# Two forward layers and their backward on one core: attention scores of four heads in one stretch instead of two pairs

## The chip, the core and the metric

The kernel runs on one core of a Trainium2 chip. A core has five engines with queues of their own: PE (TensorE, matrix products into PSUM), DVE (VectorE), ACT (ScalarE, exponentials and copies), POOL (GpSimd) and SP, which here only issues DMAs. PSUM holds eight banks of 512 float32 values on each of 128 partitions; PE writes it, DVE and ACT read it, POOL can't. The metric is the device time of the whole program in microseconds (us); lower is better.

## What is computed

The reference runs four layers on one sequence of 2048 tokens with 640 features and 32 heads of 20 features, then the gradients of everything.

```python
x = x + A(layernorm(x), A_wqkv, A_wo)      # linear attention, phi(t) = (t > 0 ? t + 1 : exp(t)) + 1e-6
x = x + B(layernorm(x), B_wqkv, B_wo)      # causal softmax attention, window of 256 tokens
x = x + A(layernorm(x), A_wqkv, A_wo)
x = x + B(layernorm(x), B_wqkv, B_wo)
out, vjp = jax.vjp(f, x, weights); return (out, *vjp(grad_out))
```

In layer B a token attends to itself and the 255 tokens before it: `scores = q k^T * 20 ** -0.5`, masked, softmax, times `v`. The change touches the forward part only.

## The kernel before

**Tiles.** A tile is 128 tokens, so there are 16. Heads are padded to 32 rows: the transposed queries and keys (`QT`, `KT`) hold four heads on the 128 partitions, 32 rows each, and eight such groups (`G = 8`). A tile's queries meet the keys of at most three tiles (`nkt`): its own block, where the mask is a triangle, the one before, unmasked, and the oldest, where the mask is the other triangle. For the first tile `nkt` is 1, for the second 2.

**Passes.** `forward()` records all its operations, each with an engine, an assumed duration, and what it reads and writes; a list scheduler (`Sched.order`) then puts them into a fixed order for each engine, by the assumed durations, a priority (the order in which they were recorded), and rings of buffers. The order is settled when the kernel is built; on the chip each engine takes its queue in order and waits at semaphores. After the first layer's chunks (`a_first(items, 0, 0)`) come two passes over all tiles, `ab_pass(0, False)` and `ab_pass(2, True)`. In one pass a tile goes through the linear-attention product (`a_num`, line 613 and the 32-column products of line 420), its output projection, a layer norm, the six query/key/value chunks of layer B (`b_qkv`), attention (`attn`), and layer B's output projection. The first pass also computes four of the six chunks of the next layer A for each tile, so it has 14 chunks a tile, the second 10. A chunk is five matmuls of 128 x 128 x 320 (line 420) into one PSUM bank of the ring `mm`, copied or added out by DVE or ACT.

**Late q.** Between the passes `late_q` computes the two query chunks of the next layer A (line 523), as fillers, with an exponential (line 528), a minimum and a maximum-plus-add on DVE (529, 531).

**Attention** works on pairs of heads. For each of 16 pairs in a tile, `products` issues 2 x `nkt` matmuls that use 32 rows of PE each (`tile_position`, line 690) into a buffer of two PSUM banks, one per head; `weights` takes one exponential over both heads (line 697, ACT), masks the own block on POOL (line 700), and the oldest block on POOL for the second pair of a group (line 704) and on DVE, by a product with `maskT_first`, for the first (line 708). `values` multiplies with the values (line 731, 2 x `nkt` matmuls of 32 columns) into a bank shared by 16 heads, which DVE normalises (738, 739).

**PSUM.** Eight banks: three single ones in ring `mm`, two buffers of two banks in ring `s`, one in `pv`. In layer 0's first stage ring `s` also takes transposes and two of the six chunks, a whole buffer each. The masked weights `e` have five buffers of two heads.

**Recording order.** The values of a pair are recorded a lag behind its scores: 2.1 sixteenths of a tile in the first pass and 3.1 in the second (`spread` in `ab_pass`).

**Copies.** Of the six chunks of layer B, ACT copies three (line 665) and DVE three (663); of the value chunks of layer A ACT copies one (476) and DVE one (479).

**Backward.** `bwd_phase` and `B_attn_bwd` follow; they use `ckv`, a small constant, at line 1495. Behind the forward the order of instructions on each engine is the same in both kernels, but for two memsets of `ckv`.

Of the kernel before, what the change touches and what calls it, by code (L numbers as in the profile page):

```python
# [11 lines left out]
ALU = mybir.AluOpType  # L12
# [188 lines left out]
class Kern:  # L201
    def __init__(self, ctx, tc, x0, A_wqkv, A_wo, B_wqkv, B_wo, grad_out, outs):
# [45 lines left out]
        self.maskT_last = self.const.tile([P, P], BF, name="maskT_last")  # L248
        self.maskT_first = self.const.tile([P, P], BF, name="maskT_first")
# [4 lines left out]
        self.mask_steps = [keep(self.maskT_last, 0, [[1, P]], -1), keep(self.maskT_first, -1, [[-1, P]], 1)]  # L254
# [8 lines left out]
        for t in (self.bmask, self.hmask, self.maskT_last, self.maskT_first):  # L263
            nc.vector.memset(t, 1.0)
        self.ckv = self.const.tile([P, 3, 4 * DH], F32, name="ckv")
        nc.vector.memset(self.ckv[:, 0:2, :], self.c_att)
        nc.vector.memset(self.ckv[:, 2, :], 1.0)
# [69 lines left out]
    def forward(self):  # L337
# [5 lines left out]
        with ExitStack() as st:  # L343
# [5 lines left out]
            def ring(name, n, shape, dt=BF, **kw):  # L349
# [4 lines left out]
            mmp, sp_ = pool("mm_ps", 3, **PS), pool("s_ps", 2, **PS)  # L354
            R = dict(
                s=Ring(2, make=lambda: sp_.tile([P, 2, 512], F32, name="s_ps"), name="s_ps"), pv=ring("pv_ps", 1, [P, 16, 32], F32, **PS),
                mm=Ring(3, make=lambda: mmp.tile([P, 512], F32, name="mm_ps"), name="mm_ps"),
                e=ring("e_sb", 5, [P, 2, 3, P]), QT=ring("QT", 2, [P, G, P]), KT=ring("KT", 5, [P, G, P]),
# [64 lines left out]
            def turn(how, dst, src, n, r, w):  # L423
# [5 lines left out]
                if how == "s":  # L429
                    ps.make = lambda: sp_.tile([P, 16, P], BF, name="s_ps")  # L430
                else:
                    ps.make = lambda: mmp.tile([P, 8, P], BF, name="mm_ps")
# [27 lines left out]
            def a_qkv(l, tt, hnT):  # L460
# [3 lines left out]
                def chunk(ci):  # L464
                    def f():
                        kind, c0 = "qkv"[ci // 2], ci * CW
                        o = c0 - ci // 2 * D
                        ring = "s" if l == 0 and ci in (0, 2) else "mm"
                        ps = R[ring].buf()
                        if ring == "s":  # L470
                            ps.make = lambda: sp_.tile([P, 1024], F32, name="s_ps")
                        mm_chunk(ps, CW, [(lambda k=k: hnT.t[:, k, :], lambda k=k: wsb["Wqkv_A"][:, k, c0:c0 + CW],
                                           k == 0, k == DT - 1) for k in range(DT)], [key_of(hnT), ("Wqkv_A", ci)])
                        if kind == "v":
                            if ci == 4:
                                op("ACT", av(CW), lambda: nc.scalar.copy(vv[:, tt, o:o + CW], ps.t[:, 0:CW]), [ps],
                                   [("vv", tt, ci)])
                            else:
                                op("DVE", vp(CW), lambda: nc.vector.tensor_copy(vv[:, tt, o:o + CW], ps.t[:, 0:CW]),
                                   [ps], [("vv", tt, ci)])  # L480
                                dma("ACT", lambda: self.tm_view(sv["v"])[:, tt, :], lambda: vv[:, tt, :], 160 * KB,
# [1145 lines left out]
```

## Time and profile before

| | us |
|---|---|
| median of 3 runs | 2318.53 (2316.77 to 2324.01) |
| span of the profiled execution | 2322.2 |
| PE busy in that span | 2109.3 (91%) |
| DVE busy | 1455.2 (63%) |
| ACT busy | 1240.5 (53%) |
| POOL busy | 853.2 (37%) |
| forward passes, first exponential of line 697 to the last one's start | 145.7 to 435.6, and 504.3 to 760.7 |

The profile shows one execution, some microseconds apart from the runs' median. Times in it are counted from the span's start. In a table of windows each row has the stretch, its length, the busy time of each engine with its instructions in brackets, the granted PE clock (1.00 is full speed), the share of time in which the 16 DMA engines were busy, and GB/s. In a timeline a row has the start, the duration of equal instructions in a row, the engine, the line, the operation, what it writes and reads, and in square brackets the idle time before it and what ended it. In a list of waits a row has who waited for whom, the total in us, how often, and the longest.

### The profile page before, as it was taken

The numbers are of one execution on the slowest core, as the hardware profiler recorded it, in microseconds if no ns is written. First come the engines' busy times: TensorE is split into PE (matmuls) and PEld (weight loads), VectorE is DVE, ScalarE is ACT, GpSimd is POOL, SyncE is SP. The second block draws the span as 40 slices with busy tenths as digits, with TensorE's granted clock in tenths as the row PEclk, the third lists the DMA queues.
The fourth block names the chain that finished last, engine by engine and source line by source line (L and its number), as shares of the span: only waits on it lengthen the run. The fifth ranks groups of instructions, "written<-read, shape, count | busy, mean of one in ns | idle before, by whom it ended". The sixth has DMA issues, their size and how long they took to land. (4 is left out here: it accounts for less than half of the span.)

```text
span 2322.2 us, 69222 instructions
## 1 busy us (share of the span) xinstructions
PE 2109.3 (91%) x28146; PEld 1435.7 (62%) x28146; DVE 1455.2 (63%) x3089; ACT 1240.5 (53%) x2077; POOL 853.2 (37%) x1852
## 2 busy tenths in 40 slices
PE   6989999989999888989889989998899888997899
PEld 4646666655555557777756557746777775654664
DVE  6756666555554678899833439805989994443551
ACT  4638888437888158888722213314888881210330
POOL 1015555215566345555512203303555551220110
PEclk9989999889999889999999999999999999998999
DMA  7759989366776956767788789936677678878973
GB/s 258 223 129 205 207 203 201 114 168 150 158 151 172 222 138 125 134 122 135 145 179 178 175 168 211 192 104 130 125 133 131 127 145 167 191 162 188 190 154 100
DMA packets 937073, 377.93 MB, mean 163 GB/s; under 512 B 817072, under 2 KB 921136, under 8 KB 936496
## 3 DMA queue, kind: packets, MB, share of 16 engines
q1 hardware_dynamic: 856672, 299.45, 63.4%
q10 hardware_dynamic: 80080, 74.06, 10.1%
q8 instruction: 220, 3.60, 0.7%
q14 instruction: 101, 0.83, 0.1%
HBM read 115.34 MB, written 114.95 MB: 99 GB/s over the span
## 5 line engine op out<-in xcount | busy, mean ns | idle before, releaser
L1442 ACT ACTIVATE e_sb<-pair 128x768 bf16<-128x768 f32 x480 | 389.3, 812 | 112.9 <-PE pair L1422 105.5
L1457 DVE TENSOR_TENSOR ds_sb<-pair,e_sb 128x768 bf16<-128x768 f32 x480 | 436.3, 948 | 6.6 <-POOL e_sb L1446 6.6
L697 ACT ACTIVATE e_sb<-s_ps 128x768 bf16<-128x768 f32 (+2 forms) x512 | 383.8, 772 | 98.9 <-PE s_ps L690 47.0
L700 POOL TENSOR_SCALAR_AFFINE_SELECT e_sb<-e_sb 128x256 bf16<-128x256 bf16 x512 | 223.9, 438 | 451.0 <-ACT e_sb L697 436.9
L931 PE MATMUL mm_ps<-wq,dqT 128*128 128x320 bf16 x1920 | 285.5, 304 | 20.7 <-DMA dqT<-dqkv 20.1
L931 PEld LDWEIGHTS <-om 128*128 128x128 bf16 x1920 | 190.9, 100 | 171.3 <-DMA om<-o 13.4
L1449 POOL TENSOR_SCALAR_AFFINE_SELECT e_sb<-e_sb 128x256 bf16<-128x256 bf16 x448 | 182.6, 408 | 264.4 <-ACT e_sb L1442 256.0
L931 PE MATMUL mm_ps<-dqkv,om 128*128 128x480 bf16 x1280 | 272.2, 371 | 0.0
L1102 POOL TENSOR_TENSOR gw<-w,gcar 128x640 f32<-128x640 f32 x64 | 89.5, 1399 | 478.7 <-ACT w L1099 468.8
L931 PEld LDWEIGHTS <-dqT 128*128 128x128 bf16 x1920 | 186.9, 99 | 97.8 <-DMA dqT<-dqkv 22.9
L1446 POOL TENSOR_SCALAR_AFFINE_SELECT e_sb<-e_sb 128x256 bf16<-128x256 bf16 x512 | 207.3, 408 | 73.0 <-ACT e_sb L1442 71.7
L1084 ACT ACTIVATE dh<-mm_ps 128x320 f32<-128x320 f32 x128 | 56.0, 437 | 331.4 <-PE mm_ps L931 268.9
L1470 PE MATMUL dsT_ps<-ident,ds_sb 128*128 128x128 bf16 x2244 | 192.8, 223 | 29.2 <-ACT dsT L1474 25.4
L1474 ACT COPY dsT<-dsT_ps 128x768 bf16<-128x768 bf16 x240 | 191.0, 796 | 12.2 <-PE dsT_ps L1470 6.0
L1470 PEld LDWEIGHTS <-ds_sb 128*128 128x128 bf16 x2244 | 140.1, 99 | 92.5 <-issue 89.0
L690 PE MATMUL s_ps<-QT,KT 32*128 32x128 bf16 x2880 | 172.0, 222 | 8.7 <-ACT e_sb L697 5.8
L420 PE MATMUL mm_ps<-Wqkv_B,hnTB 128*128 128x320 bf16 x960 | 178.7, 306 | 0.5 <-DMA hnTB<-hnB 0.5
L1486 PE MATMUL dqvk_ps<-Ksl,dsT 128*128 128x32 bf16 x2160 | 167.3, 177 | 3.5 <-DVE dqkv L1495 3.0
L1486 PEld LDWEIGHTS <-dsT 128*128 128x128 bf16 x2880 | 156.1, 97 | 22.4 <-issue 21.8
L1490 PE MATMUL dqvk_ps<-Qsl,ds_sb 128*128 128x32 bf16 x2160 | 165.0, 176 | 0.0
L1490 PE MATMUL dqvk_ps<-dOsl,e_sb 128*128 128x32 bf16 x2160 | 165.0, 176 | 0.0
L690 PEld LDWEIGHTS <-KT 32*128 32x128 bf16 x2880 | 85.0, 94 | 117.7 <-issue 111.4
(184 smaller groups left out, 3937.6 us busy)
## 6 DMA issues: line engine op xcount, KB each, us to landing
qkvp<-qk_slab SPq DMA_DIRECT2D x32, 512.0 KB, 3.3
o<-o SPq DMA_DIRECT2D x64, 160.0 KB, 3.3
om<-o SPq DMA_DIRECT2D x20, 512.0 KB, 5.0
hn<-hn SPq DMA_DIRECT2D x64, 160.0 KB, 3.0
om<-hn SPq DMA_DIRECT2D x20, 512.0 KB, 5.0
qkvp<-v_slab SPq DMA_DIRECT2D x32, 256.0 KB, 2.5
dOpt<-slab ACTq DMA_DIRECT2D x32, 256.0 KB, 3.4
Ksl<-qkvp SPq DMA_DIRECT2D x12, 512.0 KB, 4.6
```

The lines of the kernel that those rows point to most:

```text
L690: nc.tensor.matmul(s.t[:, i, j * P:(j + 1) * P], lhsT=kTs[j].t[r, g, :], rhs=qT.t[r, g, :], start=True, stop=True, tile_position=(HPAD * h ...
L697: op("ACT", av(2 * nkt * P), lambda: nc.scalar.activation(e.t[:, :, 0:nkt, :], s.t[:, :, 0:nkt * P].rearrange("p h (i q) -> p h i q", q=P) ...
L700: op("POOL", 410, lambda: nc.gpsimd.affine_select(out=e.t[:, :, nkt - 1, :], in_=e.t[:, :, nkt - 1, :], compare_op=ALU.is_ge, fill=0.0, ba ...
L931: nc.tensor.matmul(ps.t[:, w0:w0 + width], lhsT=lhsT(), rhs=rhs(), start=start, stop=stop)
L1442: nc.scalar.activation(e, PR[h][:, :, 0:3 * P].rearrange("p i (j q) -> p i j q", q=P), ACT.Exp, scale=self.c_att)
L1446: nc.gpsimd.affine_select(out=e[:, :, j, :], in_=e[:, :, j, :], compare_op=ALU.is_ge, fill=0.0, base=0, pattern=[[0, 2], [-1, P]], channel ...
L1449: nc.gpsimd.affine_select(out=e[:, :, j, :], in_=e[:, :, j, :], compare_op=ALU.is_ge, fill=0.0, base=-1, pattern=[[0, 2], [1, P]], channel ...
L1457: nc.vector.tensor_mul(DS[n][:, hs], PR.pop(h)[:, :, 0:3 * P].rearrange("p i (j q) -> p i j q", q=P), E[n][:, hs])
L1470: nc.tensor.transpose(ps[:, i, j, :], DS[n][:, 2 * p + i, j, :], self.ident)
L1474: (nc.vector.tensor_copy if h % 2 else nc.scalar.copy)(TSB[h], TPS.pop(h))
L1486: nc.tensor.matmul(a[:, 0, hh, :], lhsT=TSB[2 * n + hh // 2][:, hh % 2, j, :], rhs=ld[g]["K"][:, k, cs], start=(i == 0), stop=(i == len(dq ...
L1490: nc.tensor.matmul(a[:, 1 + x, hh, :], lhsT=src[n][:, hh, j, :], rhs=ld[g][rhs][:, q, cs], start=(i == 0), stop=(i == len(dkv) - 1))
```

## The change

Scores of all four heads of a group are issued in one stretch of 4 x `nkt` matmuls. Three heads go into one tile of three banks (`s3`, one buffer), the fourth into a single bank (`s1`, two buffers). The exponential is split: one over three heads, one over the fourth. All masks are on POOL: own block for three heads, own block for the fourth, oldest block for all four. `maskT_first` and `maskT_last` go. The ring `mm` has two banks instead of three; in layer 0's first stage the five banks of `s3` and `s1` serve as five single buffers, for three of six chunks. The weights have three buffers of four heads. ACT's copies of layer B's chunks move to DVE, as does the one of layer A's value chunk except in layer 0. `late_q` works chunk by chunk with a single bank each. The lag is 3.1 sixteenths in both passes. `ckv` is made after the forward.

```diff
-            mmp, sp_ = pool("mm_ps", 3, **PS), pool("s_ps", 2, **PS)
+            mmp = pool("mm_ps", 2, **PS)
+            sb = pool("s3_ps", **PS).tile([P, 3, 512], F32, name="s3_ps")
+            sa = [pool(f"s1_ps{i}", **PS).tile([P, 512], F32, name=f"s1_ps{i}") for i in range(2)]
+            singles = [sb[:, 0, :], sb[:, 1, :], sb[:, 2, :]] + sa
...
-                e=ring("e_sb", 5, [P, 2, 3, P]), ...
+                s=Ring(5, tiles=singles, name="s"), s3=Ring(1, tiles=[sb], name="s3"),
+                s1=Ring(2, tiles=sa, name="s1"), pv=ring("pv_ps", 1, [P, 16, 32], F32, **PS),
+                mm=Ring(2, make=lambda: mmp.tile([P, 512], F32, name="mm_ps"), name="mm_ps"),
+                e=ring("e_sb", 3, [P, 4, 3, P]), ...
...
-                            if ci == 4:
+                            if ci == 4 and l == 0:
...
-                ps, e, p_ = R["s"].buf(), R["ee"].buf(), R["pp"].buf()
+                e, p_ = R["ee"].buf(), R["pp"].buf()
                 for ci in range(2):
+                    ps, c0 = R["s1"].buf(), ci * CW
...
-                        if ci % 2:
-                            op("DVE", vp(CW), lambda: nc.vector.tensor_copy(out(), src()), [ps, "zeros"], [key])
-                        else:
-                            op("ACT", av(CW), lambda: nc.scalar.copy(out(), src()), [ps, "zeros"], [key])
+                        op("DVE", vp(CW), lambda: nc.vector.tensor_copy(out(), src()), [ps, "zeros"], [key])
...
+                def scores(g):
+                    def f():
+                        s3, s1 = R["s3"].buf(), R["s1"].buf()
+                        def mm_s():
+                            for j in range(nkt):
+                                for hh in range(4):
+                                    r = slice(HPAD * hh, HPAD * (hh + 1))
+                                    out = s3.t[:, hh, :] if hh < 3 else s1.t
+                                    nc.tensor.matmul(out[:, j * P:(j + 1) * P], lhsT=kTs[j].t[r, g, :], rhs=qT.t[r, g, :],
+                                                     start=True, stop=True, tile_position=(HPAD * hh, 0))
+                        op("PE", 200 + 56 * nkt, mm_s, [qT] + kTs, [s3, s1])
+                        e = es[g] = R["e"].buf()
+                        op("ACT", av(3 * nkt * P), lambda: nc.scalar.activation(
+                            e.t[:, 0:3, 0:nkt, :], s3.t[:, :, 0:nkt * P].rearrange("p h (i q) -> p h i q", q=P),
+                            ACT.Exp, scale=self.c_att), [s3], [(e, 0, j) for j in range(nkt)])
+                        op("ACT", av(nkt * P), lambda: nc.scalar.activation(
+                            e.t[:, 3, 0:nkt, :], s1.t[:, 0:nkt * P].rearrange("p (i q) -> p i q", q=P),
+                            ACT.Exp, scale=self.c_att), [s1], [(e, 1, j) for j in range(nkt)])
...
+                        op("POOL", 530, lambda: own_block(0, 3), [], [(e, 0, nkt - 1)])
+                        op("POOL", 300, lambda: own_block(3, 4), [], [(e, 1, nkt - 1)])
+                        if nkt == 3:
+                            op("POOL", 640, oldest_block, [], [(e, 0, 0), (e, 1, 0)])
...
-                           [(e, j) for j in range(nkt)] + [(v, c) for v in vts for c in (4, 5)], [pv])
+                           [(e, i, j) for i in range(1 + p_) for j in range(nkt)] + [(v, c) for v in vts for c in (4, 5)], [pv])
...
-                        lag = 0.001 + part * (3.1 if last else 2.1) / (2 * G)
-                        spread(items, tt + lag, tt + lag + 1.0, [att(i, part) for i in range(2 * G)])
+                        lag = 0.001 + part * 3.1 / (2 * G)
+                        spread(items, tt + lag, tt + lag + 1.0, [att(i, part) for i in range((1 + part) * G)])
```

More of the change, by code (lines that the diff above doesn't have):

```diff
@@ L467, in f @@
                         o = c0 - ci // 2 * D
[L468 to L471, printed above, removed]
+                        ps = R["s" if l == 0 and ci in (0, 2, 4) else "mm"].buf()
                         mm_chunk(ps, CW, [(lambda k=k: hnT.t[:, k, :], lambda k=k: wsb["Wqkv_A"][:, k, c0:c0 + CW],
@@ L749, in values @@
                     return f
[L750 to L751 removed]
+                return [scores(g) for g in range(G)], [values(g, p_) for g in range(G) for p_ in (0, 1)]
             def spread(items, t0, t1, fs):
```

88 lines of the change are left out of this document (31 added, 57 removed).

## The prediction

> **What bounds the kernel now.** I read the profile page's span first, then busy times over two long stretches of full tiles, then who waited for whom there, then one timeline. The change touches the two forward passes, so everything is read from those.
>
> ```profile
> span 2322.2 us, 69222 instructions
> ```
>
> ```profile
> core 0: us, PE busy (x) PEld busy (x) DVE busy (x) ACT busy (x) POOL busy (x), PEclk, DMA share, GB/s
> 212.00:398.00 186.00, 185.22 (x2713) 113.46 (x2711) 124.29 (x355) 152.83 (x260) 98.75 (x240) 1.00 0.93 204
> 420.00:437.00 17.00, 15.87 (x186) 9.28 (x183) 6.68 (x19) 12.10 (x19) 8.36 (x21) 0.52 0.13 41
> 552.00:715.00 163.00, 160.79 (x2528) 96.54 (x2527) 93.27 (x269) 134.09 (x210) 98.10 (x240) 1.00 0.71 155
> ```
>
> The first and third stretch hold 160 of the L697 exponentials each, 16 to a tile: a tile takes 18.6 us in the first pass and 16.3 in the second. PE is busy for all of it at full clock; ACT follows with 82%. The waits of PE in the same two stretches are next to nothing, 0.7 us in ten tiles and 1.7 in ten:
>
> ```profile
> PE s_ps L690 <- ACT e_sb L697: 0.7, 2, 0.4
> ```
>
> ```profile
> PE s_ps L690 <- ACT e_sb L697: 1.7, 5, 0.5
> ```
>
> So PE alone sets these tiles. The timeline shows what on it is not arithmetic:
>
> ```profile
> 266.07 0.84 PE L420 MATMUL mm_ps<-Wo_B,oTB 128*128 128x320 bf16 x5
> ...
> 266.84 0.34 PE L690 MATMUL s_ps<-QT,KT 32*128 32x128 bf16 x6
> ...
> 267.11 0.31 PE L731 MATMUL pv_ps<-v_slab,e_sb 128*128 128x32 bf16 x6
> ...
> 267.27 0.84 PE L420 MATMUL mm_ps<-Wqkv_B,hnTB 128*128 128x320 bf16 x5
> 267.28 0.81 ACT L697 ACTIVATE e_sb<-s_ps 128x768 bf16<-128x768 f32 x1 [0.38 <-PE s_ps L690]
> ```
>
> A chunk of three 320-column matmuls lasts 0.57 at 259.84, one of five 0.84: 0.135 each, 0.675 for five. The scores should thus start at 266.745; they start at 266.84, **0.10 late**. Six of them last 0.34, one alone 0.22 (its mean on the page), so the last starts 0.12 after the first: 0.06 for each pair of row groups. The values start 0.27 after the scores, so 0.15 after the last. One stretch costs 0.10 + 0.12 + 0.15 = 0.37, of which some 0.2 is switching. Check: 16 x 0.37 scores, 16 x 0.16 values (267.11 to 267.27), 14 chunks x 0.675, 0.6 for the linear-attention products = 18.5; with ten chunks 15.8. Measured 18.6 and 16.3.
>
> **The change, part by part.** *Scores.* Two stretches of six become one of twelve. If four row groups run as the pairs do, its three steps cost the same 0.06 each: 0.10 + 0.13 + 0.15 = 0.38 instead of 0.74, 0.36 less. If only two ever run together, six steps: 0.55, 0.19 less. The trace has no four groups; I take 0.38, because the pair's two matmuls start within 0.01 us and each has a PSUM bank of its own, as the four will. A tile gains 8 x 0.36 = 2.9 us (bounds 1.5 to 2.9): PE alone would give 15.65 and 12.95. The Trainium skill (TensorE: Matmul & The Clock Gate, Measured speedup vs the span model) has four row tiles at 3.07 times one, not 4. By that the three steps cost some 0.06 more, 0.5 us a tile, an estimate, and the sum below would be 11 us smaller; no run here shows it yet.
>
> *Exponentials.* L697 takes 812 ns for 768 columns, 597 for 512, 385 for 256: 172 + 0.834 a column. 1152 columns: 1.13; 384: 0.49. Neighbours overlap (two lie in 1.52 us at 745.80, 0.10 less than the sum), so 1.13 + 0.39 replaces 2 x 0.71, nothing in sum. Leaving ACT are three copies of L665 a tile (0.43 each), and L476 in the first pass; DVE takes them at 0.47 and loses eight L708 of 0.30: -0.5 us a tile in the first pass, -1.0 in the second, so cost nothing while DVE, busy for two thirds, covers them.
>
> *Masks.* POOL takes 409 ns for 256 columns and 295 for 128 (L252): 523 for 384, 637 for 512. A group costs 1.46 instead of 3 x 0.41; 11.7 us a tile, under the period but in the chain.
>
> *The new chain.* Before, four banks in two buffers let the next scores start while an exponential ran. Now there is one three-bank buffer: the next scores wait for the three-head exponential, and the oldest-block mask waits for both exponentials. From the start of a group's last score matmul (zero): exponential at 0.31 (267.28 after 266.96), ended 1.44; next scores from 1.49 (such starts stand 0.05 behind an exponential in the trace); one-head exponential 1.34 to 1.83; POOL 1.51 to 2.87 (0.07 behind ACT, neighbours overlapping by 0.05); values from 2.93.
>
> I laid this chain along the built order of both kernels' instructions, with the PE costs above. In a first-pass tile (groups 52 to 60) the scores wait once, 0.16 (behind values of the group before and a chunk), and the values twice: 0.43, where they stand straight behind the next group's scores, and 0.58, where two groups' values follow each other. The tile ends at 16.8. In the second (193 to 201) values wait 0.30, 0.48 and 1.13, the last where scores, values and scores stand together, with 0.08 for scores: 14.8. What stands behind a waiting matmul on PE is the next chunk and then the next scores, so each wait delays ACT too.
>
> Not in that chain: a pair of layer-norm activations (0.29 + 0.20) stands between the two exponentials once or twice a tile and makes a mask later; and two chunk banks instead of three. A bank is held 0.3 + 0.49 behind its 0.675, so the two carry a chunk each 0.75 us or so against one in 1.1 to 1.2 needed, as long as DVE is free. Bounds 0 and 1.5 us a tile together; I take **0.5**, near the lower, as DVE has a quarter of its time idle. So 17.3 and 15.3.
>
> *DMA.* Nothing is added, but SP's queue carries the same issues in less time: share 0.93 in the first pass would be 1.00. PE waited for DMA 0.5 us in those twenty tiles; 0 to 0.5 a tile, inside the 0.5 above.
>
> *Elsewhere.* The first stage has seven banks in turn instead of five: -2 us (DVE is busy 48 of 68 us there; -6 to 0). The late-q chunks hold one of two single banks for 0.675 + 0.3 + 0.44 + 0.25 + 0.49, about 2.2 us, so 2.2 a tile of two chunks, where 49 matmuls of L523 (ten a tile) start in 490 to 500, 2.0 a tile: +2 (0 to +6). The two ramps (118 to 177 and 460 to 536) use chunk banks for every transpose too: +3 (0 to +8). Two masks' steps and memsets less, `ckv` after the forward: its memset waits for a store of this pass that is long done: 0.
>
> *Sum.* Eleven full tiles a pass (the others are ramps and the tails, where PE waits for ACT already): 11 x (18.6 - 17.3) + 11 x (16.3 - 15.3) = 25; with +3 elsewhere, **-22 us**: 2300 for the profiled execution, whose span of 2322.2 stands 3.7 above the runs' median of 2318.5 and inside their spread. Against the median: **2297**.
>
> **Rivals.** *PE stays the bound* (the waits vanish because slips of one group are made up in the next): 11 x 2.95 + 11 x 3.3 less 3 = 66: 2252. For it: the page's ACT is at 82%. Against: the chain's 2.93 us is longer than a tile's eighth. *Row groups go in pairs only*: tiles of 17.0 and 14.3 for PE alone, waits of 0.9 and 1.6, so 17.9 and 15.9: 11 x 0.7 + 11 x 0.4 less 3 = 9: 2310. *The two chunk banks bind*: 14 and 10 chunks wait 0.15 each where I had 0.5 a tile in all, 18.9 and 16.3: no gain, 2318 to 2322. Against it: DVE's idle. *Slower: the mask chain takes over.* Its place is the values behind each group's scores. If they come 2.93 or later after their scores in every group, not in two or three of eight, each group waits some 0.5: 8 x 0.5 - 2.9 = +1.1 a tile, 22 tiles, +24, with ramps 2346. It decides from the point where masks end later than about 3.4 us after the scores, 0.5 beyond my chain: a layer-norm pair and a DMA issue ahead of the one-head exponential would do that. For it: all masks of a group stand in one FIFO behind ACT's. *Slower: the clock.* In 420 to 437, where PE had only scores and values left, it was granted 0.52. If the waits let a quarter of a tile's 13 us run at half clock, +3.2 a tile, 2365. The Trainium skill (TensorE: Matmul & The Clock Gate, A second HAM failure mode: psum-queue depth-cycling) says short idles between PSUM-bank bursts can do so. Against: the full tiles here ran at 1.00.
>
> **How the numbers follow.** Forecast 0.44 (2280 to 2312), PE-bound 0.15, pairs 0.09, chunk banks 0.11, mask chain 0.16, clock 0.05. A measurement tells 0.3%, 7 us, from no change. Faster: the forecast's 0.42, all of the PE-bound, 0.07 of the pairs: 0.64. Same: 0.02, 0.02, and 0.11: 0.15. Slower: 0.21. The range goes from inside the PE-bound case, 2256, to inside the mask chain, 2338.
>
> **What would show it.** In the changed profile: one stretch of twelve scores with 0.12 to 0.14 between first and last start (0.30 says pairs); PE busy below its present 99% in the full tiles, with waits of values for POOL of some 1 us a tile and of scores for ACT of 0.1 to 0.3; tiles of eight groups at 17.3 and 15.3 us; granted clock 1.00. Waits of chunks for DVE above 1 us a tile, or of values above 2, make it wrong upward; none at all, downward.

## The result and the profile after

The changed kernel takes **2330.21 us** (median of 13 runs, 2322.10 to 2337.86); the kernel before, beside it, 2323.03 (13 runs, 2315.75 to 2333.97). The ratio is 1.0033, 95% interval 1.0018 to 1.0048: slower by a third of a per cent, inside the range, on the other side of the forecast of 2297.

Executions differ, and the first profile of the changed kernel caught its fastest (2322.1), so its span of 2320.4 hides the loss. A second profile, run e13 below, caught one of 2331.2, beside the median. The table takes the stages of each from the starts of the score exponentials; "ten tiles" are the fourth to the thirteenth, all of them full.

| us | before | changed | changed, e13 | e13 less before |
|---|---|---|---|---|
| to the first score exponential | 145.7 | 148.7 | 149.9 | +4.2 |
| pass 0, ten tiles | 187.1 | 193.1 | 193.2 | +6.1 |
| pass 0, its ramp and tail | 102.8 | 97.5 | 98.5 | -4.3 |
| between the passes | 68.7 | 74.8 | 74.4 | +5.7 |
| pass 2, ten tiles | 163.6 | 160.7 | 167.0 | +3.4 |
| pass 2, its ramp and tail | 92.7 | 83.6 | 83.8 | -8.9 |
| the rest (backward) | 1561.6 | 1562.0 | 1562.7 | +1.1 |
| span | 2322.2 | 2320.4 | 2329.5 | +7.3 |

The two profiles of the changed kernel differ most in pass 2's ten tiles, 6.3 us. Now the lines that answer to those shown before. The page of the changed kernel begins:

```profile
span 2320.4 us, 68635 instructions
```

Its windows over ten full tiles of each pass (stretch, length, busy times, granted clock, DMA share, GB/s; like those shown before, the first starts a tile later than the ten of the table), and then e13's pass 2:

```profile
213.00:406.00 193.00, 171.46 (x2714) 108.23 (x2714) 129.59 (x317) 135.84 (x220) 110.19 (x241) 0.97 0.97 198
554.00:715.00 161.00, 140.71 (x2547) 96.44 (x2546) 90.56 (x221) 123.95 (x181) 109.08 (x241) 0.97 0.78 160
```

```profile
557.00:723.00 166.00, 142.27 (x2516) 96.78 (x2514) 90.31 (x220) 123.08 (x180) 108.16 (x238) 0.95 0.75 153
```

PE lost 14 and 20 us of busy time, but the ten tiles of pass 0 became 6 us longer and those of pass 2 only 3 shorter (in e13 3 longer), so PE now stands idle. The granted clock is no longer 1.00. PE's waits in the first pass and in the second (who for whom, us in total, times, longest):

```profile
PE pv_ps L727 <- DVE oB L735: 5.8, 9, 0.7
PE mm_ps L611 <- DVE oA L619: 2.7, 9, 0.3
PE mm_ps L419 <- DVE pk L491: 2.6, 8, 0.3
PE pv_ps L727 <- POOL e_sb L707: 2.4, 8, 0.8
PE mm_ps L419 <- DMA hnTB<-hnB: 2.4, 3, 1.0
```

```profile
PE pv_ps L727 <- POOL e_sb L707: 10.1, 15, 1.1
PE mm_ps L419 <- DMA hnTB<-hnB: 6.7, 7, 1.9
PE mm_ps L419 <- DVE qk_slab L660: 1.3, 5, 0.3
PE s_ps L689 <- ACT e_sb L693: 0.9, 3, 0.4
```

In pass 2 the values wait for the last mask, as forecast. In pass 0 they wait mostly for VectorE, by this list. That DVE is not simply full is to be seen from its own waits in the same stretch of pass 0: it stood 57.5 us (27.3, 12.3, 9.0 and 8.9) waiting for PE's chunks.

```profile
DVE x L638 <- PE mm_ps L419: 27.3, 30, 1.4
DVE v_slab L660 <- PE mm_ps L419: 12.3, 9, 1.4
```

Each waits for the other in turn, round two chunk banks: a loop of latencies. One place of it, from the timeline of pass 0; a place like it comes once a tile:

```profile
214.98 1.13 ACT L693 ACTIVATE e_sb<-s_ps 128x1152 bf16<-128x1152 f32 x1
215.01 0.64 POOL L707 TENSOR_SCALAR_AFFINE_SELECT e_sb<-e_sb 128x512 bf16<-128x512 bf16 x1
215.02 0.72 DVE L488 TENSOR_SCALAR ee<-ee 128x320 bf16<-128x320 bf16 x1
...
215.77 0.49 DVE L491 SCALAR_TENSOR_TENSOR pk<-mm_ps,ee 128x320 bf16<-128x320 f32 x1
...
216.30 0.34 ACTq L387 DMA_DIRECT2D pk<-pk  x1
...
216.68 0.46 ACTq L387 DMA_DIRECT2D ek<-ee  x1
...
217.19 0.49 ACT L696 ACTIVATE e_sb<-s_ps 128x384 bf16<-128x384 f32 x1 [1.07 <-PE mm_ps L419]
...
217.46 0.49 DVE L735 TENSOR_TENSOR oB<-pv_ps,li 128x320 bf16<-128x320 f32 x1
...
218.00 0.63 POOL L707 TENSOR_SCALAR_AFFINE_SELECT e_sb<-e_sb 128x512 bf16<-128x512 bf16 x1
...
218.10 1.05 PE L727 MATMUL pv_ps<-v_slab,e_sb 128*128 128x32 bf16 x24 [0.66 <-DVE oB L735]
```

The three-head exponential ends at 216.11. The one-head exponential of the same group could follow, but ACT's queue is in order and holds the stores of `pk` and `ek` ahead of it, and these wait for DVE's `pk`, which ends at 216.26 behind a minimum that took 0.72 beside a mask. So L696 starts at 217.19, the last mask ends at 218.63, and the second twelve values, which need it, come behind that. The line credits the idle of L696 to a chunk that it does not read; what stood ahead in its queue were the two issues, and e12 below takes them away. PE's own wait ahead of 218.10 is for `oB`, the product that frees the one value bank: in these ten tiles 19 of 20 such starts lie 0.145 or 0.146 behind its end, whatever mask ended nearby. In e13 it is again 19 of 20, although the list of its pass 0 has the masks first (POOL 6.9 us, `oB` 5.3).

**Counted from start to start.** Busy times hide short waits, since matmul ends are modelled. So I took each interval between neighbouring matmul starts in the trace, subtracted what the same pair takes unhindered (0.135 for 320 columns, 0.10 ahead of scores, 0.147 behind them), and put the excess to the instruction whose end stands just before. For ten tiles of the first profile:

| us, ten tiles | pass 0 before | pass 0 changed | forecast | pass 2 before | pass 2 changed | forecast |
|---|---|---|---|---|---|---|
| PE without waits | 183.6 | 155.4 | 156.5 | 156.5 | 128.3 | 129.5 |
| for POOL and ACT (score and mask chain) | 1.4 | 7.4 | 11.5 | 2.2 | 16.7 | 18.5 |
| for DVE | 0.0 | 20.7 | 5 | 1.5 | 5.0 | 5 |
| for DMA and the like | 0.0 | 3.9 | 0 | 1.1 | 5.5 | 0 |
| excess at half clock | 0.0 | 4.4 | 0 | 0.0 | 3.7 | 0 |
| under 0.03 each | 2.1 | 1.3 | | 2.2 | 1.2 | |

The 20.7 are 7.7 for `oB` (the value bank) and 13.0 for products that free a chunk bank: `oA` 4.6, `pk` 3.7, `qk_slab` 2.6, `x` 2.1. Counted in the same way, pass 0 of e13 has 20 us for DVE too, and 11.5 for the masks in place of 7.4.

### The profile page after: what moved, and what is told of

Same layout as the page of the kernel before. It is cut to its first block, busy times and chain, and to the rows that moved or that the text cites. A ratio compares the mean times of both kernels' runs of the same rounds, so it can differ in the third digit from the quotient of the medians.

```text
span 2320.4 us, 68635 instructions
## 1 busy us (share of the span) xinstructions
PE 2044.7 (88%) x28146; PEld 1415.6 (61%) x28146; DVE 1463.6 (63%) x3007; ACT 1199.1 (52%) x1981; POOL 881.1 (38%) x1850
## 5 line engine op out<-in xcount | busy, mean ns | idle before, releaser
L702 POOL TENSOR_SCALAR_AFFINE_SELECT e_sb<-e_sb 128x384 bf16<-128x384 bf16 (+1 forms) x512 | 198.3, 408 | 420.5 <-ACT e_sb L693 402.2
L693 ACT ACTIVATE e_sb<-s_ps 128x1152 bf16<-128x1152 f32 (+2 forms) x256 | 274.1, 1071 | 132.1 <-PE s_ps L689 109.9
L1444 POOL TENSOR_SCALAR_AFFINE_SELECT e_sb<-e_sb 128x256 bf16<-128x256 bf16 x448 | 182.4, 407 | 266.2 <-ACT e_sb L1437 257.6
L1441 POOL TENSOR_SCALAR_AFFINE_SELECT e_sb<-e_sb 128x256 bf16<-128x256 bf16 x512 | 207.1, 408 | 72.8 <-ACT e_sb L1437 71.5
L1465 PE MATMUL dsT_ps<-ident,ds_sb 128*128 128x128 bf16 x2244 | 193.0, 223 | 29.1 <-ACT dsT L1469 25.5
L1469 ACT COPY dsT<-dsT_ps 128x768 bf16<-128x768 bf16 x240 | 191.0, 796 | 12.5 <-PE dsT_ps L1465 6.3
L1485 PE MATMUL dqvk_ps<-Qsl,ds_sb 128*128 128x32 bf16 x2160 | 165.0, 176 | 0.0
L1485 PE MATMUL dqvk_ps<-dOsl,e_sb 128*128 128x32 bf16 x2160 | 165.0, 176 | 0.0
L727 PE MATMUL pv_ps<-v_slab,e_sb 128*128 128x32 bf16 x2880 | 128.6, 178 | 38.9 <-POOL e_sb L707 26.8
L727 PEld LDWEIGHTS <-e_sb 128*128 128x128 bf16 x2880 | 105.1, 97 | 82.9 <-POOL e_sb L707 49.7
```

What stands on the lines that cost most here:

```text
L693: op("ACT", av(3 * nkt * P), lambda: nc.scalar.activation(e.t[:, 0:3, 0:nkt, :], s3.t[:, :, 0:nkt * P].rearrange("p h (i q) -> p h i q", q=P),
L702: nc.gpsimd.affine_select(out=v, in_=v, compare_op=ALU.is_ge, fill=0.0, base=0, pattern=[[0, h1 - h0], [1, P]], channel_multiplier=-1)
L727: nc.tensor.matmul(pv.t[:, h % 16, :], lhsT=e.t[:, hh, j, :], rhs=vts[j].t[:, h, :], start=(j == 0), stop=(j == nkt - 1))
L1441: nc.gpsimd.affine_select(out=e[:, :, j, :], in_=e[:, :, j, :], compare_op=ALU.is_ge, fill=0.0, base=0, pattern=[[0, 2], [-1, P]], channel ...
L1444: nc.gpsimd.affine_select(out=e[:, :, j, :], in_=e[:, :, j, :], compare_op=ALU.is_ge, fill=0.0, base=-1, pattern=[[0, 2], [1, P]], channel ...
L1465: nc.tensor.transpose(ps[:, i, j, :], DS[n][:, 2 * p + i, j, :], self.ident)
```

## The experiments

Two theories stood at first. **A**: the two chunk banks with a fuller DVE hold PE. **B**: the values wait for the longer chain of two exponentials and up to three masks. Lines are those of the changed kernel unless the text says "before". All ratios are to the kernel before on the same chip, with 95% intervals; tiles are ten full ones of one profiled execution.

One reservation holds for all of these runs: the list scheduler orders all queues anew for every edit, and part of a difference can come from that order. In the ten tiles PE's order is that of the changed kernel in both passes of e13 and in pass 0 of e9; e3, e11, e12 and e17 share one order in pass 0, which differs from the changed kernel's in one place a tile. In pass 2, e3, e11 and e17 share an order that is quite another than the changed kernel's. (Where an expectation speaks of a lag in "tenths", sixteenths of a tile are meant.)

| run | pass 0 | between | pass 2 | time | ratio |
|---|---|---|---|---|---|
| before | 187.1 | 68.7 | 163.6 | 2323.03 | 1 |
| changed | 193.1 | 74.8 | 160.7 | 2330.21 | 1.0033 (1.0018 to 1.0048) |
| e1 three chunk banks | 186.8 | 116.7 | 174.1 | 2412.45 | 1.0385 (1.0359 to 1.0411) |
| e2 copies back on ACT | 196.9 | 71.4 | 165.3 | 2331.56 | 1.0042 (1.0024 to 1.0061) |
| e3 oldest mask in two parts | 192.5 | 72.5 | 152.4 | 2311.80 | 0.9936 (0.9911 to 0.9961) |
| e4 no masks | 196.7 | 79.3 | 161.1 | 2326.11 | 1.0002 (0.9982 to 1.0021) |
| e5 late q on five banks | 194.7 | 51.9 | 170.0 | 2324.45 | 1.0002 (0.9987 to 1.0017) |
| e6 e1 with e3 and late q | 194.3 | 50.1 | 177.8 | 2366.14 | 1.0176 (1.0152 to 1.0201) |
| e7 before, two chunk banks | 190.7 | 67.1 | 172.4 | 2336.10 | 1.0041 (1.0025 to 1.0056) |
| e8 before, masks on POOL | 190.9 | 65.9 | 165.3 | 2327.39 | 1.0010 (0.9995 to 1.0026) |
| e9 weight transposes later | 189.8 | 77.6 | 169.5 | 2343.11 | 1.0091 (1.0067 to 1.0114) |
| e10 before, the same | 187.3 | 68.2 | 165.0 | 2322.52 | 1.0004 (0.9990 to 1.0017) |
| e11 e3, transposes, late q | 184.5 | 76.8 | 150.1 | 2308.50 | 0.9945 (0.9925 to 0.9966) |
| e12 e3, issues on SP | 196.2 | 71.3 | 151.3 | 2321.34 | 1.0003 (0.9987 to 1.0019) |
| e13 changed again | 193.2 | 74.4 | 167.0 | 2331.19 | 1.0035 (1.0019 to 1.0051) |
| e14 before, stretch alone | 192.4 | 64.8 | 185.7 | 2360.10 | 1.0149 (1.0130 to 1.0168) |
| e15 the same, lag 2.1 in pass 0 | 196.9 | 70.5 | 184.1 | 2372.66 | 1.0202 (1.0184 to 1.0220) |
| e16 e14 with masks on POOL | 193.1 | 67.6 | 175.5 | 2352.05 | 1.0135 (1.0104 to 1.0165) |
| e17 e3 again | 193.0 | 73.3 | 146.6 | 2309.77 | 0.9938 (0.9913 to 0.9962) |

### e1 to e4: banks, copies, masks

e1 gives the third bank back to the chunks, and takes one of the fourth head's two:

```diff
-            mmp = pool("mm_ps", 2, **PS)
+            mmp = pool("mm_ps", 3, **PS)
...
-            sa = [pool(f"s1_ps{i}", **PS).tile([P, 512], F32, name=f"s1_ps{i}") for i in range(2)]
+            sa = [pool(f"s1_ps{i}", **PS).tile([P, 512], F32, name=f"s1_ps{i}") for i in range(1)]
...
```

> The changed kernel with three chunk banks (mm) and one bank for the fourth head (s1) instead of two and two; its first stage has four single buffers in turn instead of five, and the late-q chunks share the one s1 bank. Theory A (the gain of the four-head stretch is given back because two chunk banks and a fuller DVE make chunks wait): the waits of chunks for DVE in the full tiles, 12.8 us in ten tiles of the first pass and 5.1 in ten of the second, nearly go, some 15 us in both passes; the late-q stretch gets worse by up to 10, so the whole is 0 to 15 us below the changed kernel (2315 to 2330). Theory B (it is given back because values wait for the longer chain of exponential, exponential and masks): the waits for POOL, 14.1 and 15.3 us in the same tiles, stay or grow, and as scores now wait for the one-head exponential as well, tiles do not get shorter: 2330 to 2345.

Pass 0 fell to 186.8: waits for DVE went from 20.7 us to 0.5. But the scores then wait for ACT, 16 us in pass 0 by the count of starts: 7.7 ahead of a stretch, for the three-head exponential, and 8.4 inside it, where the fourth head has a single bank and waits for the one-head exponential (25 starts, all 0.050 or 0.051 behind its end). Pass 2 waits 27.8 us for POOL, and `late_q`, with one bank, took 42 us more between the passes, with half the clock for 72 us on end there:

```profile
PE s_ps L521 <- DVE pp L529: 29.9, 22, 2.3
```

So the waits for DVE go when a third bank is there, as theory A has it for pass 0, and most of them come back as waits for ACT; PE's order is another as well. The bank is not to be had for nothing.

e2 puts back ACT's copies:

```diff
-                            if ci == 4 and l == 0:
+                            if ci == 4:
...
-                        op("DVE", vp(CW), lambda: nc.vector.tensor_copy(out(), src()), [ps, "zeros"], [key])
+                        if ci % 2:
+                            op("DVE", vp(CW), lambda: nc.vector.tensor_copy(out(), src()), [ps, "zeros"], [key])
+                        else:
+                            op("ACT", av(CW), lambda: nc.scalar.copy(out(), src()), [ps, "zeros"], [key])
```

> The changed kernel with the three even layer-B chunks copied by ACT again, and the first value chunk of layer A too, so DVE has 1.4 to 1.9 us a tile less. Theory A: chunks wait less for DVE, half of the 12.8 and 5.1 us goes: 5 to 10 us faster than the changed kernel (2320 to 2325). Theory B: the copies stand between the exponentials in ACT's queue, masks come later, values wait more: 0 to 8 us slower (2330 to 2338).

No gain: in pass 0 DVE's 20.7 became 15.7, and 13.0 us of waits of scores for ACT took the place; in pass 2 the waits for POOL grew from 15.3 to 21.6.

e3 cuts the oldest mask in two, so that its first part follows the three-head exponential (`oldest_block` takes the heads as `own_block` does):

```diff
                         op("POOL", 530, lambda: own_block(0, 3), [], [(e, 0, nkt - 1)])
+                        if nkt == 3:
+                            op("POOL", 530, lambda: oldest_block(0, 3), [], [(e, 0, 0)])
                         op("POOL", 300, lambda: own_block(3, 4), [], [(e, 1, nkt - 1)])
                         if nkt == 3:
-                            op("POOL", 640, oldest_block, [], [(e, 0, 0), (e, 1, 0)])
+                            op("POOL", 300, lambda: oldest_block(3, 4), [], [(e, 1, 0)])
```

> The changed kernel with the oldest block's mask in two parts, three heads straight behind the own block of these three, then the fourth head's two masks, so the first half of a group's values needs only the first exponential: by the durations of the profile it is ready some 0.4 us earlier, the second half 0.2 later. Theory B: the waits of values for POOL in the full tiles fall from 14.1 and 15.3 us to about half, 8 to 15 us faster than the changed kernel (2315 to 2322). Theory A: chunk waits stay and take up what is freed: 0 to 3 us faster (2327 to 2330).

This is the first version that beats both kernels, 0.64% under the kernel before, and again 0.62% in e17. POOL does more (119.95 instead of 109.08 us in ten tiles), and the values of the first pair no longer wait for the one-head exponential: in pass 2 the first six values of 68 of the 80 groups start ahead of the last mask of their group, by 0.4 us at the median, where in the changed kernel none did and 34 started 0.04 to 0.075 behind it. In the list of pass 2 the first wait came down from 10.1:

```profile
PE pv_ps L729 <- POOL e_sb L707: 4.2, 10, 0.7
```

Pass 0, in nearly the same order, did not move: there the chain is not the first wait. In pass 2 the order is a new one: PE has 26 runs of twelve values and 108 of six, the changed kernel 64 and 32. So the wait of theory B is real in pass 2; how much of the 8.3 us is the split mask's and how much the new order's is not shown.

e4 is the changed kernel without its three mask operations (both of `own_block` and `oldest_block`), so that attention is over whole blocks:

> The changed kernel without any mask in the forward attention (both triangles are left out, so the attention is over whole blocks); POOL has nothing to do in the passes. Theory B: values wait for the exponentials alone, 1.0 us earlier: the 14.1 and 15.3 us of waits for POOL go, and with the tails some 30 us: 2300. Theory A: the chunks wait as before and most of the freed time turns into waits for DVE: at most 10 us faster: 2320 to 2330.

Little came of it, 4 us, or 0.3% by the ratios. In pass 0 the values then wait for the one-head exponential itself; the scores of pass 2, again in another order, wait for ACT 10.6 us:

```profile
PE pv_ps L723 <- ACT e_sb L696: 10.4, 8, 2.9
```

It also settles the long minimum. The row of L488 in ten tiles of pass 0, first of the changed kernel, then without masks (the last number ahead of the second bar is the mean in ns):

```profile
L488 DVE TENSOR_SCALAR ee<-ee 128x320 bf16<-128x320 bf16 x20 | 10.7, 535 | 1.1 <-ACT ee L487 1.0
```

```profile
L488 DVE TENSOR_SCALAR ee<-ee 128x320 bf16<-128x320 bf16 x20 | 4.8, 239 | 16.1 <-ACT ee L487 16.1
```

With POOL idle it takes 239 ns; the 535 beside masks are a mean of unlike ones. Twelve of the 20 start 0.01 to 0.04 behind a mask of 0.64 and take 0.69 to 0.72; seven start 0.46 behind one and take 0.27; all nineteen end 0.09 to 0.10 after that mask. One starts ahead of its mask and takes 0.244, and that mask takes 0.69. The Trainium skill (SBUF — State Buffer, Who interferes with whom) says that a `tensor_scalar` of VectorE in a two-port mode and a GpSimd instruction shut each other out for the whole instruction. The trace agrees: at 215.02 the minimum starts 0.01 after a mask of 0.64 and ends 0.09 behind that mask's end.

### e5 and e6: the late query projection

e5 puts `late_q` on the ring of five single banks, issuing each chunk in one piece; e6 is e1 with e3 and the same on four banks. In both, nothing keeps the late query chunks and the scores of the same banks apart, so part of the query products is overwritten; the times tell of the order of work only.

```diff
-                    ps, c0 = R["s1"].buf(), ci * CW
-                    for k0, k1 in ((0, 2), (2, DT)):
+                    ps, c0 = R["s"].buf(), ci * CW
+                    for k0, k1 in ((0, DT),):
```

> The changed kernel with its late query projection put on the ring of five single score banks instead of the two one-bank buffers of head four (and each half chunk issued in one piece). Theory A (too few banks per chunk, so that PE waits for the vector engine's exponential-minimum-maximum chain there): the stretch between the passes, 74.8 us after against 68.7 before, falls to 66 to 69 us, the tiles stay at 193 and 161 us per ten, and the time falls by 6 to 9 us to 2321 to 2324. Rival (the chain on ScalarE and VectorE sets that stretch, not the banks): within 2 us of 74.8 and of the changed kernel's time.

> The changed kernel with three chunk banks (one buffer left for head four), the oldest mask in two parts after each exponential, and the late query projection on the four single score banks. If the chunk banks set pass 0 and the masks pass 2: ten tiles of pass 0 at 183 to 187 us (two banks and split masks: 192.5), of pass 2 at 163 to 168 (with one buffer for head four the scores of the next group wait for the one-head exponential, 174.1 without the split), the stretch between at 66 to 70: together within 4 us of 2306. If the chunk waits only move to another engine, as when the masks were left out: pass 0 at 190 or more and a time of 2315 or more.

In e5 the time fell by 6 us, as A had it, but not where it had it: the stretch between came down to 51.9, and part was given back in the passes (pass 2's tiles 170.0, pass 0's 194.7). In e11, with the order kept, the stretch stays at 76.8; so the gain is not shown for a kernel that keeps it. e6 missed by 60: by the count of starts PE waits for ACT 19 us in ten tiles of pass 0 and 24 in pass 2, 11 and 17 of them for the one-head exponential, and for POOL 16.3 in pass 2. One buffer for head four costs more than the third chunk bank brings, whatever `late_q` does.

### e7 and e8: the parts in the kernel before

e7 makes three chunk banks two (`pool("mm_ps", 2)`, `Ring(2`); e8 moves the product with `maskT_first` to a POOL mask:

```diff
-                    if nkt == 3 and p_ == 1:
+                    if nkt == 3:
-                    elif nkt == 3:
-                        op("DVE", v2(2 * P), lambda: nc.vector.tensor_mul(
...
```

> The kernel before with two chunk banks instead of three and nothing else changed. Theory A (two chunk banks by themselves make PE wait for VectorE): the 13.0 and 5.1 us of such waits that the changed kernel has in its twenty full tiles come back here, and the ends add a few: 2335 to 2345 us. Theory B (two banks cost only where the score stretch got shorter and VectorE fuller): at most 5 us over 2323, and ten tiles of pass 0 at 187 to 190.

> The kernel before with the oldest mask of both head pairs on POOL (no multiplication by a mask on VectorE). VectorE loses 25 us per ten tiles of pass 0 in 312-ns products, POOL gains as many masks; the minimum on ee, 281 ns before, gets longer. If mask work on POOL hurts by itself: 5 us or more over 2323. If it only hurts where the values wait for it (five buffers of one pair each cover it here): within 3 us of 2323.

Two banks alone cost 3.6 us in ten tiles of pass 0 and 8.8 in pass 2: 0.6 a tile, near the forecast's 0.5, for that kernel. Only 3.3 us of PE's new waits in pass 0 are for DVE, not the 13.0 of the changed kernel: so in these two kernels the banks bind more where PE is quicker. In pass 2, where PE's order is a new one, the list has ACT's exponentials (5.7) and `oB` (2.6) instead of chunks. The time rose by 11 us, as theory A had it. Masks on POOL alone cost +3.8 and +1.7 in the tiles and nothing that the time can tell.

### e9, e10 and e12: the queues

DMA's share of 0.97 in pass 0 suggested a third theory, **D**, that DMA sets those tiles. e9 and e10 make the twenty weight transposes of layer A follow `late_q`:

```diff
+                    if tag == "A":
+                        keys.append(("pqT", min(i, TT - 1)))
```

> The changed kernel with its twenty transposing loads of the layer A weights (wT from Wqkv_A and Wo_A, which run among the full tiles of pass 0) made to follow the late query projection, so that they fall between the passes and into the start of pass 2. Theory D (DMA, at a share of 0.97 in the full tiles of pass 0, sets them once PE has room): ten tiles of pass 0 fall from 193 to 180 to 186 us, the rest gives back at most 3, and the time falls by 5 to 10 us, to 2320 to 2325. Rival (the chains through POOL and VectorE set those tiles; the share is high because transfers linger): within 2 us of 193, time within 3 us of 2330.

> The same edit on the kernel before, as a control. PE is busy 185.2 of 186 us there, so under both theories ten tiles of pass 0 stay at 186 to 188 us; the time stays within 3 us of 2325, and DMA's share of those tiles falls from 0.93 to about 0.75.

The share fell from 0.97 to 0.81, the tiles from 193.1 to 189.8: D explains 3 us of pass 0, between the two expectations, with PE's order unchanged. The transposes then delayed pass 2's (PE's waits for `hnTB` 12.5 us instead of 6.7), and the backward part took 1569.8 instead of 1562.0 and 1562.7. The control stayed in its bounds, at a share of 0.74.

e12 is e3 with the stores of `pk`, `ek`, `v`, `o`, `r` and `linv` issued by SP (`dma("ACT", ...)` made `dma("SP", ...)` on seven lines):

> The changed kernel with the oldest mask in two parts, and the stores of pk, ek, v, o, r and linv issued from SP instead of ScalarE, on whose queue they stand between the exponentials and wait for VectorE. If that queueing sets the tiles of pass 0: 192.5 us per ten fall to 185 to 189, and the time from 2311.8 to 2304 to 2308. If not (or if SP, which carries the transposing loads, becomes late): within 2 us of 192.5 or more, and 2311 or more.

The row of L696 in ten tiles of pass 0, first of the changed kernel (in e3 its idle time is 15.3), then of e12 (idle time stands behind the second bar):

```profile
L696 ACT ACTIVATE e_sb<-s_ps 128x384 bf16<-128x384 f32 x80 | 38.8, 485 | 11.8 <-PE mm_ps L419 8.5 <-DVE st L447 2.1 <-DMA WqTA<-wT 1.1
```

```profile
L696 ACT ACTIVATE e_sb<-s_ps 128x384 bf16<-128x384 f32 x80 | 38.7, 484 | 0.0
```

PE's waits for POOL in pass 0 went from 7.0 (e3) to 1.3, in the same order of PE. But SP's queue, which carries the transposing loads, now waits for DVE in its turn: waits for DMA went from 3.2 to 9.6, for `oB` from 7.8 to 12.8, and the backward part took 1575.5 (1562.6 and 1567.5 in e3 and e17). The issues do hold ACT, and moving them moves the wait. In one place it paid: the time to the first score exponential is 140.9 us, against 148.2 in e3 and 145.7 in the kernel before.

### e11: together

e3 and e9, and `late_q` in an order that keeps the banks apart: odd tiles on `s3`, even ones on the two of `s1`.

```diff
+                wide = R["s3"].buf() if tt % 2 else None
...
-                    ps, c0 = R["s1"].buf(), ci * CW
+                    c0 = ci * CW
+                    one = None if wide else R["s1"].buf()
+                    ps = (wide, ci) if wide else one
```

> The changed kernel with three edits: the oldest mask in two parts, the weight transposes later, and the late query projection on all five score banks in an order that keeps them apart (odd tiles on the three-bank buffer, even tiles on the two single ones). If the three gains are separate ones (mask chain in pass 2, DMA in pass 0, two banks between the passes): 2311.8 less 5 to 10 for the transposes less 2 to 6 between the passes, 2296 to 2305. If all of them only uncover the same static order: 2308 to 2314.

Pass 0 got to 184.5, the best of all, and the time not beyond e3's: the stretch between gave back 4 us, and the backward part, at 1566.0, lay 3 above e3's profile (e17's was 1567.5). The three gains are not separate ones. PE's order in both passes is e3's, so pass 0 can be compared directly: the split mask alone took 0.6 us off it, the later transposes alone 3.3, both together 8.6.

### e13 to e17: the stretch alone

e13 is the changed kernel and e17 is e3, both run again. e14 puts the stretch alone into the kernel before, with values 3.1 sixteenths behind their scores in both passes; e15 and e16 start from e14. The edit of e14, without its two lines on the lag:

```diff
                         for j in range(nkt):
-                            for i, hh in enumerate((2 * p_, 2 * p_ + 1)):
+                            for hh in range(4):
...
-                                nc.tensor.matmul(s.t[:, i, j * P:(j + 1) * P], lhsT=kTs[j].t[r, g, :],
+                                nc.tensor.matmul(ss[hh // 2].t[:, hh % 2, j * P:(j + 1) * P], lhsT=kTs[j].t[r, g, :],
...
+                        ss = [R["s"].buf(), R["s"].buf()]
+                        products(g, ss)
+                        for p_ in (0, 1):
+                            weights(g, p_, ss[p_])
```

> The changed kernel once more, for a second profile and for its time on the same chip as the next two runs. If the forward stages set its median, this profile, when it lies nearer to 2330 than the first (2320.4), shows the missing us in the tiles of the two passes (193.1 and 160.7 us per ten in the first) or in more windows of half clock; if they are in the backward part, that part is above 1562 us.

> The kernel before with one edit: the scores of four heads in one stretch of twelve 32-row matmuls into both two-bank score buffers (so that the next group waits for both exponentials), values recorded 3.1 tenths behind the scores in both passes as in the changed kernel; three chunk banks, copies on ScalarE and VectorE in turn, masks and five buffers of a pair as before. If the other parts of the change cost the gain: PE alone needs 15.65 and 12.95 us a tile, ScalarE is busy 15.3 and 13.4, so ten tiles at 165 to 178 and 142 to 152 us, and 2295 to 2310. If the scores wait for the exponentials of the group before them (one set of score banks): 187 or more and 160 or more, and 2320 or more.

> The same with the lags of the kernel before (2.1 tenths in pass 0, 3.1 in pass 2), so that in pass 0 the values stand nearer to their scores in PE's order. If the values' place in the order decides: pass 0 at 5 us or more per ten tiles above the run with 3.1; if not, within 2 us of it. Pass 2 is recorded the same and stays within 2 us.

> The kernel before with the stretch of twelve matmuls (values 3.1 tenths behind) and with all masks on POOL, by pairs; three chunk banks and the copies as before. If the mask product in VectorE's queue is what made the stretch alone slower: the 17.4 and 16.2 us per ten tiles of such waits go, less some 3 us of waits for POOL: ten tiles at 175 to 182 and 155 to 172 us and 2320 to 2335; below the changed kernel's 2330 only if the two chunk banks cost more than the wait for both exponentials. If the values wait as long for POOL instead: 188 or more, 180 or more, and 2350 or more.

> The changed kernel with the oldest mask in two parts, once more: 2308 to 2315 if the gain of 0.64% over the kernel before holds on another chip, with ten tiles of pass 2 at 150 to 156 us and of pass 0 at 190 to 194.

e13 shows the median's missing us in pass 2's ten tiles (DMA 7.2 instead of 5.5, half clock 6.5 instead of 3.7, ACT 2.5 instead of 1.4). e14 is the surprise: the stretch alone costs 35 us, inside its second expectation, but mostly by another wait. The values wait, in ten tiles of each pass, for the mask product in DVE's queue:

```profile
PE pv_ps L732 <- DVE e_sb L708: 18.3, 28, 1.9
```

```profile
PE pv_ps L732 <- DVE e_sb L708: 17.9, 28, 0.9
PE s_ps L690 <- ACT e_sb L697: 9.8, 24, 0.5
```

e15 loses 4.5 us more in pass 0's tiles, between the 2 that were to say that the values' place in PE's order doesn't count and the 5 that were to say that it decides. e16 takes the product away, and the scores wait for the exponentials in its place, in pass 0 and in pass 2:

```profile
PE s_ps L690 <- ACT e_sb L697: 21.9, 37, 2.5
```

```profile
PE s_ps L690 <- ACT e_sb L697: 26.1, 60, 0.5
```

The time came out 17 us above my bound: I had priced the product's wait and not the one behind it. So the stretch by itself doesn't bring the gain that the other parts then spoil: those parts make it bearable. Which of them does (the fifth bank for scores, the exponential in two, the copies away from ACT) was not tried one by one.

## Why the prediction was wrong

**Right.** The stretch. At the median its twelve matmuls start 0, 3, 7, 10, then 66 to 77, then 122 to 132 ns after the first, in three steps of four, and the next instruction follows 0.28 after the first. With 0.10 ahead that is 0.38, as taken, and PE without waits came down by 28.2 us in ten tiles of either pass, 2.8 a tile where I had 2.9. The Trainium skill's 3.07 for four row tiles (TensorE: Matmul & The Clock Gate, Measured speedup vs the span model), measured there at 512 columns, is not seen here at 128: a step of four takes what a step of two took. Durations came as interpolated: exponentials of 1131 and 485 ns for 1.13 and 0.49, the mask of 512 columns 637 for 637. The chain was nearly right in size (7.4 and 16.7 us in ten tiles where I had 11.5 and 18.5).

**Wrong: the 0.5 a tile for two chunk banks and a fuller DVE.** In pass 0 it measured 2.1 a tile, 20.7 us in ten, four times as much and beyond my upper bound of 1.5. I had set it near the lower bound "as DVE has a quarter of its time idle". DVE kept a third of its time idle and PE waited for it all the same: the reason counted throughput, and what binds is the round trip chunk, copy, bank, in queues that stand in order. e1 shows it from one side (third bank, waits for DVE gone in pass 0), e7 from the other (two banks bind little in pass 0 while PE sets the pace). The sign that I had named for it came, with waits of chunks for DVE above 1 us a tile: 13.0 in ten. And 7.7 of the 20.7 were not for a chunk bank: the one value bank, freed by `oB` behind layer-norm work in DVE's queue, was not in my list.

**Left out.** Waits for DMA, 3.9 and 5.5, which I had put inside the 0.5; and the clock, 4.4 and 3.7. In the twenty tiles of the kernel before no window of half clock lies; in the changed one's there are six of 3.4 us. My clock rival had the mechanism and eight times the price. The Trainium skill (TensorE: Matmul & The Clock Gate, A second HAM failure mode: psum-queue depth-cycling) names short idles between groups of matmuls as a cause. That the windows lie in tiles with waits agrees, but waits alone don't bring them: pass 0 of e11, with 16% of its time in waits, has none; and no run isolates the cause. Together: 16 for DVE, 9 for DMA, 8 for the clock, less 6 for the chain, are 27 of the 28 us by which the twenty tiles (353.8) missed 326.

**Wrong in the ends.** The first stage was to gain 2 and lost 3 to 4: PE waits there 9.7 us for ACT's copy of a value chunk (`vv`, L472), which stands on a score bank. e12 takes the stores out of ACT's queue, and there, with the same banks, this wait is 0.9 and the stage 7.8 us shorter than in the changed kernel: that queue held the copies up. `late_q` cost 6, the top of my bounds. The ramps and tails gained 13 to 14 where I had a loss of 3, or a loss of 1 with the eleventh full tile that the table counts among them. No run tested the ramps. Together the ends came out 2 to 5 us shorter where I had about 1 longer: that misses of +5, +4 and -14 largely cancel is luck. It is luck too that the time lies inside the range, whose slow end I had drawn from the mask chain alone.

**Of the rivals**, the two chunk banks were nearest, at 0.11. The mask chain is the first wait in pass 2 only: e3, which shortens it, has 8.3 us less in its ten tiles, in a new order, and 0.6 less in pass 0's.

**What stays open.** Which of DVE's, ACT's and SP's orders would let pass 0 go under 184.5. In e2, e4 and e12 the relief of one wait there was taken up by the next; only two together (e11) went clearly below the kernel before. Whether another recorded order, or moving the stores in the first stage alone, would do better was not tried.

## What to carry to other kernels

In this kernel one engine was full and the others busy for two thirds, and work saved on the full one turned into waits for the others' round trips. So price the loop (produce, wait, drain, free the buffer) by latency, with all that stands ahead in each queue, DMA issues among it; the idle share said nothing of it here. Before cutting the full engine's work, list every single buffer that it writes (here the value bank) and who frees it. When a chain crosses two engines, let its first part go as soon as its own input is there: with one mask cut in two, a loss of 0.3% became a gain of 0.6%. And where a scheduler settles the order, compare the order before crediting an edit: it is part of the edit.

## What the runs showed of the hardware

A minimum over 128x320 bf16 on VectorE took 239 ns with POOL idle. Behind a POOL mask that had already started it ended 0.09 to 0.10 us after that mask, and so took up to 720 ns; ahead of one it took 244, and the mask became longer (0.69 instead of 0.64). Four 32-row matmuls of 128 columns into four banks started within 10 ns of each other, and three steps of four took what three steps of two took (the next instruction 0.279 and 0.272 behind the first). PE's granted clock fell to half for 3.4 us at a time in tiles where about a fifth of the time was waits, six times in twenty tiles, and never in the twenty of the kernel before, where PE was full; no threshold follows, as pass 0 of e11 had 16% and no such window.
